# P x V of a head pair in one group of 32-column products on shared PSUM banks, with 64-row scores for the first three pairs

## The chip, the cores and the metric

The kernel runs on one core of one Trainium2 chip. The metric is the device time of one execution in microseconds (us); the time before is the median of three runs, 1092.33 us (1091.08 to 1095.45).

## The reference

Attention with a soft cap on the scores, then two feed-forward layers over all tokens, all in float32:

```python
scores = cap * np.tanh(scale * (q @ k.T) / cap)      # 4 x 12 heads, 448 tokens, 64 wide
attn = np.exp(scores - max); attn /= attn.sum(-1) + 1e-09
x = (attn @ v)  # heads side by side: 1792 x 768
h = x @ w_in                    # 768 -> 2048
x = (h * np.cos(h)) @ w_out     # 2048 -> 768
a = x @ w1; b = x @ w2          # 768 -> 1024 each
out = ((a * b) @ w3) @ w_out2   # 1024 -> 1024 -> 768
```

## The kernel before

The 48 heads are handled as 24 pairs; the two heads of a pair share one 128-row tile. The scores are computed transposed: keys lie on the partitions, in four chunks of 112, and the 448 queries along the free axis. TensorE multiplies in a one-pass float32 form, so an operand that needs full precision is split into a high and a low part. For that `a_load` loads each head's 64 rows of q and k twice, into the upper and the lower half of the partitions, and `a_split` makes of them `qh`, `ql` and `ks` (high part of k above, low part below), so that one product over 128 rows gives two terms at once. `c_S` makes two chunks of one head: two matmuls per chunk, into one of two double PSUM banks (`double`). `c_exp` runs tanh and exp on ScalarE, 112 x 896 each, into a `p` tile. `c_PV` takes the `p` tiles of both heads for half of the chunks: P x V with 64-column weights, the two heads in the two column halves of one bank, then the sums of the exponentials with a 32-column tile of ones, four side by side, in another bank. These products are plain float32; each stands as two instructions in the trace. `c_move` evicts both banks, `c_sums` sends the sums through DRAM to spread their reciprocals over the partitions, `c_norm` multiplies, and `a_out` splits the result for the first feed-forward layer.

Beside attention, TensorE computes `w3 @ w_out2` ahead of its use (`make_w34`, weights `w3h`, `w2h` and their low parts) and, later, the first layer (`moe1`). Those weights come as float64 words; `convert` turns them into float32: a scaling of the high words (line 861 on ScalarE or 862 on GpSimd, whichever the planner finds free), a step on GpSimd or DVE, then two bit operations on DVE (lines 874 and 878).

The order of all instructions is set by a planner (`Plan.schedule`): each step has a due time, the engines it may run on with a cost for each, and the buffers that it needs from rings. A ring hands its buffers out in the order in which its users were written down. For PSUM there are rings of two double banks for scores, one bank for P x V, one for the sums, and two (`hy_r`) for everything else. The order that the planner finds is then fixed for each engine; an instruction waits where what it needs is not there. One queue, SP's, issues all DMAs. All matmuls of `mm3` stand at lines 383 to 385, all tensor subtractions and additions of DVE at 369, copies at 359 (ScalarE) and 360 (DVE), DMAs at 379.

Of the kernel before, what the change touches and what calls it, by code (L numbers as in the profile page):

```python
# [11 lines left out]
F32 = mybir.dt.float32  # L12
# [7 lines left out]
P = 128  # L20
B, H, S, D = 4, 12, 448, 64
CP = 112
# [113 lines left out]
class Plan:  # L136
# [57 lines left out]
    def schedule(self):  # L194
# [23 lines left out]
        while done < len(self.ops):  # L218
# [4 lines left out]
            idle = {e for e in free if free[e] <= t + 1e-9}  # L223
            wait, rest, again = {}, [], False
            for c in cands:
# [6 lines left out]
                if pick[0] in idle and port(pick) and free["port"] > t + 1e-9:  # L232
                    pick = None
                elif pick[0] not in idle:
                    if len(o.opts) == 1:
                        wait[pick[0]] = wait.get(pick[0], 0.0) + pick[1] * PAR["back"]
                    pick = None
                if pick is None or any(it.slot is None and it.first is not o for it in o.uses if it.ring) or any(
                        it.ring.queue[0] is not it or not it.ring.free or it.ring.free[0][0] > t + 1e-9
                        for it in o.allocs):  # L240
                    rest.append(c)
                    continue
                for it in o.allocs:
                    it.ring.queue.pop(0)
                    it.slot = heapq.heappop(it.ring.free)[1]
# [88 lines left out]
def program(  # L334
# [70 lines left out]

    class Banks(Ring):
        def __init__(self, slots):
# [6 lines left out]
    class Doubles(Banks):  # L414
        def tile(self, k):
            return doubles[k]

    class Scratch:
# [7 lines left out]
        def at(self, sub, pick=None):  # L426
            return Ref(self.item, sub, pick)
# [76 lines left out]
    if general:  # L504
        tiles += [
            ("vr", [CP, NC, D], F32, 2), ("vs", [CP, NC, 2, D], F32R, 3), ("t", [CP, S], F32, G["nt"]), ("sm", [CP, 2, NC], F32, 4),
            ("rs", [CP, 2, NC], F32, 3), ("rb", [P, S], F32, 1),
            ("ph", [CP, S], F32R, G["nph"]), ("pl", [CP, S], F32R, G["npl"]),
        ]
    else:  # L510
        tiles += [("v", [CP, 2, NC, D], F32, 2), ("ones", [CP, Q], F32, 1)]
        tiles += [("p", [CP, 2, S], F32, 4), ("xs", [P, S], F32, 2), ("zs", [P, S], F32, 2), ("rs", [P, 2, S // D], F32, 2), ("rb", [P, S], F32, 1)]
    for tag, shape, dtype, n in tiles:
# [38 lines left out]

    def a_out(i, g):

        if i % 2 == 0:
            return
        b, h = divmod(i, H)
        kk = h // 2
        x = Ref(x32.pop(i // 2))
        if general:  # L560
            tt(at(g), x, Ref(rb.pop(i // 2)), x, S, ALU.mult, "PD")
# [6 lines left out]
        copy(at(g), th, x, S, "PAD")  # L568
        lo(at(g), tl, x, th, S)
        if b >= BH:  # L570
            for d, t in zip(xB_d, (th, tl)):
                z = d.at((b, kk), lambda d: d[b - BH, kk])
                dma(at(g + 1), z, t.view(lambda x: x.bitcast(F32)), r=[t], w=[z], kb=230, write=True)

# [17 lines left out]

    NT = NC // 2

    def c_consts():
# [11 lines left out]

    def c_S(i, c, g):
        qh, ql, ks = st[i]
        s = s_t[i, c] = s_r.ref()  # L610

        def f():
            for n in range(2):
                o, w = s()[:CP, n, :S], ks()[:, (2 * c + n) * CP:(2 * c + n + 1) * CP]
# [3 lines left out]
        plan.op(at(g), [("PE", 4 * MM, f)], r=st[i], w=[s])  # L618

    def c_exp(i, c, g):  # L620
        s = s_t.pop((i, c))[:CP, :, :S]
        p = ph_t[i, c] = A["p"].ref()
        for f, x, o in ((AF.Tanh, ts, s), (AF.Exp, pac, p)):
            plan.op(at(g), [("ACT", 0.144 + 2 * S / 1200,
                             lambda f=f, x=x, o=o: ACT.activation(o(), s(), f, scale=x[:CP]))],  # L625
                    r=[s], w=[o], table="exp")

    def c_PV(n, c, one, g):
        ps = [ph_t.pop((2 * n + j, c)) for j in range(2)]
        if c == 0:  # L630
            pv_t[n], zs_t[n] = pv_r.ref(), z_r.ref()
        pv, z, w = pv_t[n], zs_t[n], Ref(vt[n])
        flags = dict(start=c == 0, stop=c == NT - 1)
# [11 lines left out]
        plan.op(at(g), [("PE", 3 * 4 * MM, f)], r=[w, one, *ps], w=[pv, z])  # L645

# [26 lines left out]

    def c_norm(n, g):
        x32[n] = A["x32"].new()
        tt(at(g), Ref(x32[n]), pv_t.pop(n), Ref(rb[n]), S, ALU.mult, "DP")

# [5 lines left out]
    def columns():  # L683
        one = c_consts()
        a_load(0, -2)
        a_split(0, -1)
        for g in range(-8, NT * NH + 16):
            of_pair(a_load, -G["ql"], g, NT)
            of_head(cv_load, -2, g, NT)
            of_pair(a_split, -G["qs"], g, NT)  # L690
            if 0 <= g < NT * NH:
                n, k = divmod(g, 2 * NT)
                c, j = divmod(k, 2)
                c_S(2 * n + j, c, g)
                c_exp(2 * n + j, c, g)
# [8 lines left out]
        plan.move(pv_r, hy_r, at(g))  # L704
        plan.move(z_r, hy_r, at(g))

# [113 lines left out]
    def queries():  # L820
        a_load(0, -2)
        a_split(0, -1)
        for g in range(-8, NC * NH + 24):
# [14 lines left out]
            of_head(a_R, 8, g, NC)  # L838
            of_head(a_out, 17, g, NC)
            if g == NC * G["hsw"] + 11:  # L840
# [12 lines left out]

    def convert(due, raw_r, x, src, n):

# [26 lines left out]

    def f64(due, raw_r, x_r, src, n, hi, lw, spill=None):

        x = x_r.ref()[:, :n]
        convert(due, raw_r, x, src, n)
# [20 lines left out]
    def make_w34():  # L907
# [12 lines left out]
        for k, (fc, p) in enumerate(runs):  # L920
# [4 lines left out]
            w3 = pair(w3_r)  # L925
            f64(due - G["e3"] * (k == 0), raw_r, x_r, w3T[fc, :, p * F2:(p + 1) * F2], F2 // 2, *w3)
            for n, jc in enumerate(new):
                wo[jc] = pair(w2_r)
                f64(due - (G["e2"] - n * G["e1"]) * (k == 0), raw_r, x_r, w_out2[jc], DM, *wo[jc])
            for n in range(2):  # L930
# [423 lines left out]
```

## Time and profile before

| | before |
|---|---|
| median of three runs | 1092.33 us |
| the profiled execution, its own time | 1093.39 us |
| its span, first to last instruction | 1091.1 us |
| granted TensorE clock, mean share | 0.997 |
| busy: PE, DVE, ScalarE, GpSimd | 1064.5, 869.6, 502.1, 161.1 us |
| moved by DMA | 169.17 MB |

The page names TensorE's matmuls PE and its weight loads PEld, VectorE DVE, ScalarE ACT, GpSimd POOL. Matmuls overlap and their ends are modelled, so the step from one start to the next tells what a matmul costs, not its duration. In the window view, each stretch has busy time and number of instructions for each engine, the granted clock as a share of the full one, the busy share of the DMA engines and the rate in GB/s. In the timeline, a row has a start, a duration, what ran, and in brackets how long the engine was idle before it and what ended that.

### The profile page before, as it was taken

The numbers are of one execution on the slowest core, as the hardware profiler recorded it, in microseconds if no ns is written. First come the engines' busy times: TensorE is split into PE (matmuls) and PEld (weight loads), VectorE is DVE, ScalarE is ACT, GpSimd is POOL, SyncE is SP. The second block draws the span as 40 slices with busy tenths as digits, with TensorE's granted clock in tenths as the row PEclk, the third lists the DMA queues.
The fourth block names the chain that finished last, engine by engine and source line by source line (L and its number), as shares of the span: only waits on it lengthen the run. The fifth ranks groups of instructions, "written<-read, shape, count | busy, mean of one in ns | idle before, by whom it ended". The sixth has DMA issues, their size and how long they took to land.

```text
span 1091.1 us, 14889 instructions
## 1 busy us (share of the span) xinstructions
PE 1064.5 (98%) x5424; PEld 892.4 (82%) x5424; DVE 869.6 (80%) x1336; ACT 502.1 (46%) x661; POOL 161.1 (15%) x154
## 2 busy tenths in 40 slices
PE   5999999999999999999999999999999999999997
PEld 3666766677767777779999999998999999999996
DVE  6888767698978988969889977779799879667643
ACT  5788767787666656632244221112333236221121
POOL 2222111122312311111001110001223100000000
PEclk9999999999999999999999999999999999999999
DMA  8796876767756655425643422104655436321232
GB/s 244 200 221 181 231 209 174 219 208 223 219 161 197 188 171 166 153 84 193 223 141 119 147 58 59 58 15 136 223 188 203 141 104 226 119 87 59 59 96 95
DMA packets 83268, 169.17 MB, mean 155 GB/s; under 512 B 19698, under 2 KB 56562, under 8 KB 83186
## 3 DMA queue, kind: packets, MB, share of 16 engines
q1 hardware_dynamic: 83186, 168.14, 51.0%
q8 instruction: 44, 0.72, 0.3%
q14 instruction: 38, 0.31, 0.1%
HBM read 129.30 MB, written 38.62 MB: 154 GB/s over the span
## 4 chain that ended last, share of the span: by engine, by line
PE 90%; DVE 6%; ACT 2%; DMA 1%; issue 1%; SPq 0%; POOL 0%; DVEq 0%; POOLq 0%; ACTq 0%
PE bank L383 25%; PE bank L384 24%; PE bank L385 24%; PE bank L639 6%; PE double L615 3%; PE bank L643 3%; PE double L616 3%; DVE y L369 1%; DVE w L369 1%; DMA wi_d<-wx 1%; ACT double L625 1%; DVE kk L1008 0%; ACT p L625 0%; DMA kr<-in_k 0%; DVE g L369 0%
## 5 line engine op out<-in xcount | busy, mean ns | idle before, releaser
L383 PE MATMUL bank<-g,woh 128*128 128x448 f32 x384 | 140.8, 367 | 4.1 <-DVE y L369 3.5
L384 PE MATMUL bank<-g,woh 128*128 128x448 f32 x384 | 139.4, 363 | 0.9 <-DVE g L369 0.9
L383 PE MATMUL bank<-xh,wih 128*128 128x448 f32 x384 | 140.2, 365 | 0.0
L369 DVE TENSOR_TENSOR y<-bank,y 128x448 f32<-128x448 f32 x168 | 103.5, 618 | 45.7 <-PE bank L385 44.5
L385 PE MATMUL bank<-xh,wil 128*128 128x448 f32 x384 | 139.3, 363 | 0.0
L385 PE MATMUL bank<-g,wol 128*128 128x448 f32 x384 | 139.3, 363 | 0.0
L384 PE MATMUL bank<-xl,wih 128*128 128x448 f32 x384 | 139.2, 363 | 0.0
L359 ACT COPY hs<-bank 128x448 f32<-128x448 f32 x77 | 41.2, 535 | 200.9 <-PE bank L385 200.7
L625 ACT ACTIVATE double<-double,ts 112x896 f32<-112x896 f32 x96 | 94.0, 981 | 69.4 <-PE double L616 69.1
L625 ACT ACTIVATE p<-double,pac 112x896 f32<-112x896 f32 x96 | 96.6, 1012 | 1.8
L383 PEld LDWEIGHTS bank<-g,woh 128*128 128x128 f32 x384 | 71.9, 187 | 20.1 <-DVE y L369 6.2
L615 PE MATMUL double<-qh,ks 128*112 128x448 f32 x192 | 72.6, 378 | 13.9 <-DVE ks L369 9.6
L383 PEld LDWEIGHTS bank<-xh,wih 128*128 128x128 f32 x384 | 71.9, 187 | 16.0 <-issue 8.0
L639 PE MATMUL bank<-p,v 112*64 112x448 f32 x384 | 84.1, 558 | 0.0
L384 PEld LDWEIGHTS bank<-g,woh 128*128 128x128 f32 x384 | 72.1, 188 | 6.4 <-DVE g L369 1.3
L384 PEld LDWEIGHTS bank<-xl,wih 128*128 128x128 f32 x384 | 72.1, 188 | 5.2
L385 PEld LDWEIGHTS bank<-g,wol 128*128 128x128 f32 x384 | 72.1, 188 | 4.2
L385 PEld LDWEIGHTS bank<-xh,wil 128*128 128x128 f32 x384 | 72.1, 188 | 4.2
L616 PE MATMUL double<-ql,ks 128*112 128x448 f32 x192 | 72.3, 376 | 0.0
L384 PE MATMUL bank<-ab,w34h 128*128 128x448 f32 x192 | 69.7, 363 | 0.0
L383 PE MATMUL bank<-ab,w34h 128*128 128x448 f32 x192 | 69.7, 363 | 0.0
L385 PE MATMUL bank<-ab,w34l 128*128 128x448 f32 x192 | 69.3, 361 | 0.0
(224 smaller groups left out, 2304.4 us busy)
## 6 DMA issues: line engine op xcount, KB each, us to landing
rawc<-in_w_out SPq DMA_DIRECT2D x16, 768.0 KB, 5.1
stq<-w_d SPq DMA_DIRECT2D x32, 384.0 KB, 3.3
qr<-in_q SPq DMA_DIRECT2D x48, 224.0 KB, 4.2
kr<-in_k SPq DMA_DIRECT2D x48, 224.0 KB, 4.5
rawc<-in_w_in SPq DMA_DIRECT2D x13, 768.0 KB, 5.4
raw<-in_w3T SPq DMA_DIRECT2D x16, 512.0 KB, 5.9
rawl<-in_w SPq DMA_DIRECT2D x10, 768.0 KB, 4.7
raw<-in_w_out SPq DMA_DIRECT2D x8, 768.0 KB, 7.3
```

Of the source, the lines that this page charges most:

```text
L359: "A": ("ACT", (0.051 if psum else 0.094) + n / 1200, lambda: ACT.copy(dst(), src())),
L369: "D": ("DVE", 0.068 + n / 960, lambda: DVE.tensor_tensor(dst(), a(), b(), op=op))
L383: PE.matmul(out, wh, xh, start=first, stop=False, skip_group_check=on)
L384: PE.matmul(out, wh, xl, start=False, stop=False, skip_group_check=on)
L385: PE.matmul(out, wl, xh, start=False, stop=last, skip_group_check=on)
L615: PE.matmul(o, w, qh(), start=True, stop=False)
L616: PE.matmul(o, w, ql(), start=False, stop=True)
L625: lambda f=f, x=x, o=o: ACT.activation(o(), s(), f, scale=x[:CP]))],
L639: PE.matmul(pv()[j * D:(j + 1) * D, :S], w()[:, j, 2 * c + k], p()[:, k, :], **first)
L643: PE.matmul(z()[q:q + Q, :S], one(), p()[:, k, :], **flags)
```

## The change

`c_PV` takes the whole pair (both halves) as one step from pair 2 on; pairs 0 and 1 keep two halves. The P x V weights of a head are cut into two pieces of 32 columns, so that P x V and the sums have the same tile shape, four side by side. The banks of P x V and of the sums come from one ring of four with all other products (`hy_r`); that ring is "loose": a user may take a buffer out of the written order, if enough are free and no user with an earlier due time goes short. There are six `p` tiles in place of four. For the first three pairs (`SLIM`), q and k are loaded once, without the duplicate, and split at half the length; `c_S` then makes one chunk of both heads, three terms of 64 rows for each head, the heads in the two row halves and in the two banks of a double bank. The first weights' scaling may only run on GpSimd (`early`). Normalizing and its followers have other due times.

```diff
 class Ring:
+    loose = False
...
+                need = {}
+                for it in o.allocs:
+                    need[it.ring] = need.get(it.ring, 0) + 1
+                lack = {r for r, n in need.items() if sum(x[0] <= t + 1e-9 for x in r.free) < n}
                 if pick is None or any(it.slot is None and it.first is not o for it in o.uses if it.ring) or any(
-                        it.ring.queue[0] is not it or not it.ring.free or it.ring.free[0][0] > t + 1e-9
-                        for it in o.allocs):
+                        not r.loose and r.queue[0].first is not o for r in need) or lack or short & need.keys():
+                    short |= {r for r in lack if r.loose}
                     rest.append(c)
...
-        s_r, pv_r, z_r, hy_r = Doubles((0, 1)), Banks((4,)), Banks((5,)), Banks((6, 7))
+        s_r, hy_r = Doubles((0, 1)), Banks((4, 5, 6, 7))
...
-        tiles += [("p", [CP, 2, S], F32, 4), ...
+        tiles += [("p", [CP, 2, S], F32, 6), ...
...
+    SLIM = 3
+
+    def c_load(i, g):
+        if i // 2 >= SLIM:
+            return a_load(i, g)
+        b, h = divmod(i, H)
+        qk[i] = A["qr"].new(), A["kr"].new()
+        for it, src in zip(qk[i], (q2, k2)):
+            r = it.at(0, lambda t: t[:, 0])
+            dma(at(g) if i else -99.0, r, lambda src=src: src[b, h // 2], w=[r], kb=230)
+
+    def c_split(i, g):
...
+        copy(at(g), kh, k, S, "PAD")
+        lo(at(g), kl, k, kh, S)
+        copy(at(g), qh, q, S, "PAD")
+        lo(at(g), ql, q, qh, S)
+        st[i] = (kh, qh), (kh, ql), (kl, qh)
...
+    def c_S(n, k, g):
+        s = s_t[n, k] = s_r.ref()
+        if n < SLIM:
+            terms = st[2 * n]
+
+            def f():
+                for m, (w, x) in enumerate(terms):
+                    for j in range(2):
+                        r = slice(j * D, (j + 1) * D)
+                        PE.matmul(s()[:CP, j, :S], w()[r, k * CP:(k + 1) * CP], x()[r], start=m == 0, stop=m == 2)
...
-    def c_PV(n, c, one, g):
+    def c_PV(n, cs, one, g):
...
-            for k in range(2):
-                first = dict(start=c == 0 and k == 0, stop=c == NT - 1 and k == 1)
-                for j, p in enumerate(ps):
-                    PE.matmul(pv()[j * D:(j + 1) * D, :S], w()[:, j, 2 * c + k], p()[:, k, :], **first)
-            for j, p in enumerate(ps):
-                for k in range(2):
-                    q = Q * (2 * j + k)
-                    PE.matmul(z()[q:q + Q, :S], one(), p()[:, k, :], **flags)
+            for c in chunks:
+                flags = dict(start=c == 0, stop=c == NC - 1)
+                for q in range(P // Q):
+                    j, d = divmod(q * Q, D)
+                    PE.matmul(pv()[q * Q:(q + 1) * Q, :S], w()[:, j, c, d:d + Q], piece(j, c), **flags)
+            for c in cs:
+                for j in range(2):
+                    for k in range(2):
+                        q = Q * (2 * j + k)
+                        PE.matmul(z()[q:q + Q, :S], one(), piece(j, 2 * c + k), start=c == 0, stop=c == NT - 1)
...
-            if g >= 3 and g % 2 and g - 3 < NT * NH:
-                c_PV((g - 3) // (2 * NT), (g - 3) % (2 * NT) // 2, one, g)
+            of_two(lambda n, g: n < 2 and c_PV(n, [0], one, g), 3, g)
+            of_two(lambda n, g: c_PV(n, [1] if n < 2 else [0, 1], one, g), 5, g)
...
-            of_two(c_norm, 10, g)
-            of_head(a_out, 9, g, NT)
+            of_two(lambda n, g: c_norm(n, at(g) + 11), 6, g)
+            of_two(lambda n, g: a_out(2 * n + 1, at(g) + 14), 6, g)
...
-    def convert(due, raw_r, x, src, n):
+    def convert(due, raw_r, x, src, n, early=False):
...
-        ], r=[r], w=[r])
+        ][early:], r=[r], w=[r])
```

How the order moves shows at three places. In the names, the number behind a tile is its buffer; `bank_75` to `bank_78` are the four single banks, `double_82` and `double_83` the double ones.

TensorE, the P x V step of a pair after the start. Before, one half of pair 3, and the product behind it:

```order
L639 MATMUL bank_75<-p_153,v_128 64x448
L639 MATMUL bank_75<-p_157,v_128 64x448
L639 MATMUL bank_75<-p_153,v_128 64x448
L639 MATMUL bank_75<-p_157,v_128 64x448
L643 MATMUL bank_76<-p_153,ones_109 32x448 x2
L643 MATMUL bank_76<-p_157,ones_109 32x448 x2
L383 MATMUL bank_78<-w2h_210,w3h_159 128x384
```

In the changed kernel, the whole pair 2 (its sums stand as eight rows, of which two are shown):

```order
L694 MATMUL bank_77<-p_180,v_119 32x448 x4
L694 MATMUL bank_77<-p_196,v_119 32x448 x4
L694 MATMUL bank_77<-p_271,v_119 32x448 x4
L694 MATMUL bank_77<-p_276,v_119 32x448 x4
L699 MATMUL bank_78<-p_180,ones_109 32x448
L699 MATMUL bank_78<-p_196,ones_109 32x448
```

The two halves of a pair, which stood apart with other products between them, are one run of 16 and 8 products; all have 32 columns, and the banks are no longer always 75 and 76.

TensorE, around the first score tiles of pair 1. Before, the second pair of weight products stands ahead of them:

```order
L383 MATMUL bank_77<-w2h_210,w3h_159 128x384
L384 MATMUL bank_77<-w2l_226,w3h_159 128x384
L385 MATMUL bank_77<-w2h_210,w3l_171 128x384
L383 MATMUL bank_78<-w2h_210,w3h_159 128x384
L384 MATMUL bank_78<-w2l_226,w3h_159 128x384
L385 MATMUL bank_78<-w2h_210,w3l_171 128x384
L615 MATMUL double_82<-qh_205,ks_208 112x448
L616 MATMUL double_82<-ql_216,ks_208 112x448
```

In the changed kernel:

```order
L650 MATMUL double_83<-qh_202,ks_205 112x448 x2
L650 MATMUL double_83<-ql_226,ks_205 112x448 x2
L650 MATMUL double_83<-qh_202,ks_205 112x448 x2
L389 MATMUL bank_77<-w2h_223,w3h_165 128x384
L390 MATMUL bank_77<-w2l_247,w3h_165 128x384
L391 MATMUL bank_77<-w2h_223,w3l_176 128x384
L389 MATMUL bank_78<-w2h_223,w3h_165 128x384
L390 MATMUL bank_78<-w2l_247,w3h_165 128x384
L391 MATMUL bank_78<-w2h_223,w3l_176 128x384
L650 MATMUL double_82<-qh_202,ks_205 112x448 x2
```

The six weight products have moved behind the first two score tiles, to the place ahead of the third.

GpSimd, its first steps on weights (`raw` is what was loaded, `x` the converted tile). Before:

```order
L867 TENSOR_SCALAR x_143<-raw_115 128x512
L862 TENSOR_SCALAR raw_117<-raw_117 128x768
L867 TENSOR_SCALAR x_165<-raw_117 128x768
L862 TENSOR_SCALAR raw_119<-raw_119 128x768
L867 TENSOR_SCALAR x_143<-raw_119 128x768
L867 TENSOR_SCALAR x_165<-raw_115 128x768
```

In the changed kernel:

```order
L914 TENSOR_SCALAR raw_113<-raw_113 128x512
L919 TENSOR_SCALAR x_148<-raw_113 128x512
L914 TENSOR_SCALAR raw_115<-raw_115 128x768
L919 TENSOR_SCALAR x_167<-raw_115 128x768
L914 TENSOR_SCALAR raw_117<-raw_117 128x768
L919 TENSOR_SCALAR x_148<-raw_117 128x768
```

The scaling ahead of the first `x` step, which ScalarE did, now stands on GpSimd as well.

## Rows read from the trace of the kernel before

**Rows 1.** The page's table of engines: busy us, share of the span, instructions.

```profile
PE 1064.5 (98%) x5424; PEld 892.4 (82%) x5424; DVE 869.6 (80%) x1336; ACT 502.1 (46%) x661; POOL 161.1 (15%) x154
```

**Rows 2.** Busy time by stretch, from two questions to the window view.

```profile
0.00:45.00 45.00, 30.33 (x135) 17.52 (x136) 29.89 (x40) 27.74 (x37) 11.88 (x15) 0.96 0.80 229
45.00:200.00 155.00, 155.00 (x867) 105.66 (x869) 118.47 (x181) 118.62 (x146) 25.56 (x29) 1.00 0.77 199
200.00:490.00 290.00, 285.69 (x1468) 214.41 (x1460) 248.21 (x368) 188.78 (x216) 64.63 (x57) 1.00 0.60 183
...
225.00:255.00 30.00, 29.98 (x155) 23.46 (x154) 28.29 (x41) 25.42 (x32) 7.36 (x6) 1.00 0.76 233
```

**Rows 3.** Timeline of PE around one P x V block.

```profile
164.56 0.34 PE L385 MATMUL bank<-w2h,w3l 128*128 128x384 f32 x1
164.83 1.72 PE L639 MATMUL bank<-p,v 112*64 112x448 f32 x8
166.48 0.96 PE L643 MATMUL bank<-p,ones 112*32 112x448 f32 x8
167.37 0.45 PE L383 MATMUL bank<-w2h,w3h 128*128 128x384 f32 x1
167.65 0.34 PE L384 MATMUL bank<-w2l,w3h 128*128 128x384 f32 x1
167.83 0.34 PE L385 MATMUL bank<-w2h,w3l 128*128 128x384 f32 x1
```

**Rows 4.** Timeline inside the same block, weight loads, and one piece of PE.

```profile
165.26 0.14 PEld L639 LDWEIGHTS bank<-p,v 112*64 112x64 f32 x2 [0.23 <-issue]
165.63 0.14 PEld L639 LDWEIGHTS bank<-p,v 112*64 112x64 f32 x2 [0.23 <-issue]
...
166.01 0.55 PE L639 MATMUL bank<-p,v 112*64 112x448 f32 x2
...
166.48 0.15 PEld L643 LDWEIGHTS bank<-p,ones 112*32 112x32 f32 x7 [0.70 <-issue]
```

**Rows 5.** Timeline of the start, all engines.

```profile
1.19 1.38 SPq L379 DMA_DIRECT2D qr<-in_q  x2
...
5.79 0.63 DVE L360 CAST qh<-qr 128x896 fp32r<-128x896 f32 x1 [1.38 <-DMA qr<-in_q]
...
7.81 0.63 DVE L360 CAST ks<-kr 128x896 fp32r<-128x896 f32 x1 [0.27 <-DMA kr<-in_k]
8.48 1.09 DVE L369 TENSOR_TENSOR ks<-kr,ks 64x896 fp32r<-64x896 f32 x1
...
9.62 0.72 PE L615 MATMUL double<-qh,ks 128*112 128x448 f32 x1 [9.62 <-DVE ks L369]
10.02 0.67 ACT L861 ACTIVATE raw<-raw 128x512 f32<-128x512 f32 x1 [5.37 <-DMA raw<-in_w3T]
...
10.51 0.58 PE L615 MATMUL double<-qh,ks 128*112 128x448 f32 x1
...
10.88 0.58 PE L616 MATMUL double<-ql,ks 128*112 128x448 f32 x1
...
11.49 0.98 ACT L625 ACTIVATE double<-double,ts 112x896 f32<-112x896 f32 x1 [0.81 <-PE double L616]
```

**Rows 6.** Timeline of PE in the stretch of pair 1.

```profile
26.15 0.45 PE L384 MATMUL bank<-w2l,w3h 128*128 128x384 f32 x1 [0.97 <-DVE w2l L369]
...
27.57 0.36 PE L616 MATMUL double<-ql,ks 128*112 128x448 f32 x1
27.77 0.37 PE L615 MATMUL double<-qh,ks 128*112 128x448 f32 x1
...
31.24 0.45 PE L615 MATMUL double<-qh,ks 128*112 128x448 f32 x1 [2.09 <-ACT p L625]
...
33.81 2.64 PE L639 MATMUL bank<-p,v 112*64 112x448 f32 x8
```

**Rows 7.** Waits of PE from 200 to 490 us: total, times, longest.

```profile
PE bank L383 <- DVE y L369: 3.5, 5, 1.2
```

More of the change, by code (lines that the diff above doesn't have):

```diff
@@ L223, in schedule @@
             idle = {e for e in free if free[e] <= t + 1e-9}
-            wait, rest, again = {}, [], False
+            wait, rest, again, short = {}, [], False, set()
             for c in cands:
@@ L243, in schedule @@
                 for it in o.allocs:
-                    it.ring.queue.pop(0)
+                    it.ring.queue.remove(it)
                     it.slot = heapq.heappop(it.ring.free)[1]
@@ L406, in program @@
     class Banks(Ring):
+        loose = not general
         def __init__(self, slots):
@@ L551, in a_split, with a_out @@
             st[i + j] = qh[:, j], ql[:, j], ks[:, j]
-    def a_out(i, g):
+    def a_out(i, due):
         if i % 2 == 0:
@@ L560, in a_out @@
         if general:
-            tt(at(g), x, Ref(rb.pop(i // 2)), x, S, ALU.mult, "PD")
+            tt(due, x, Ref(rb.pop(i // 2)), x, S, ALU.mult, "PD")
         if b < BH:
@@ L567, in a_out @@
             th, tl = A["xsh"].ref(), A["xsl"].ref()
-        copy(at(g), th, x, S, "PAD")
-        lo(at(g), tl, x, th, S)
+        copy(due, th, x, S, "PAD")
+        lo(due, tl, x, th, S)
         if b >= BH:
@@ L572, in a_out @@
                 z = d.at((b, kk), lambda d: d[b - BH, kk])
-                dma(at(g + 1), z, t.view(lambda x: x.bitcast(F32)), r=[t], w=[z], kb=230, write=True)
+                dma(due + 3, z, t.view(lambda x: x.bitcast(F32)), r=[t], w=[z], kb=230, write=True)
     def of_head(f, lag, g, n):
@@ L593, in program @@
     NT = NC // 2
+    SLIM = 3
[8 more added lines that the diff above has]
+    def c_split(i, g):
+        if i // 2 >= SLIM:
+            return a_split(i, g)
+        q, k = (x.at(0, lambda t: t[:, 0]) for x in qk.pop(i))
+        qh, ql, ks = (A[x].new() for x in ("qh", "ql", "ks"))
+        kh, kl = (ks.at(j, lambda t, j=j: t[:, j]) for j in range(2))
+        qh, ql = (x.at(0, lambda t: t[:, 0]) for x in (qh, ql))
+        copy(at(g), kh, k, S, "PAD")
[3 more added lines that the diff above has]
+        st[i] = (kh, qh), (kh, ql), (kl, qh)
     def c_consts():
@@ L606, in cv_load, with c_exp @@
         dma(at(g), r, lambda: v[b, h], w=[r])
-    def c_S(i, c, g):
-        qh, ql, ks = st[i]
-        s = s_t[i, c] = s_r.ref()
+    def c_S(n, k, g):
[7 more added lines that the diff above has]
+                        PE.matmul(s()[:CP, j, :S], w()[r, k * CP:(k + 1) * CP], x()[r], start=m == 0, stop=m == 2)
+            plan.op(at(g), [("PE", 3 * MM + 0.3, f)], r=[y for x in terms for y in x], w=[s])
+            return
+        c, j = divmod(k, 2)
+        qh, ql, ks = st[2 * n + j]
         def f():
-            for n in range(2):
-                o, w = s()[:CP, n, :S], ks()[:, (2 * c + n) * CP:(2 * c + n + 1) * CP]
+            for m in range(2):
+                o, w = s()[:CP, m, :S], ks()[:, (2 * c + m) * CP:(2 * c + m + 1) * CP]
                 PE.matmul(o, w, qh(), start=True, stop=False)
                 PE.matmul(o, w, ql(), start=False, stop=True)
[L618 to L622, printed above, removed]
+        plan.op(at(g), [("PE", 4 * MM, f)], r=st[2 * n + j], w=[s])
+    def c_exp(n, k, g):
+        s = s_t.pop((n, k))[:CP, :, :S]
+        p = A["p"].ref()
+        for j in range(2):
+            if n < SLIM:
+                ph_t[n, j, k] = p, j
+            else:
+                ph_t[n, k % 2, k // 2 * 2 + j] = p, j
         for f, x, o in ((AF.Tanh, ts, s), (AF.Exp, pac, p)):
@@ L626, in c_exp, with piece @@
                     r=[s], w=[o], table="exp")
-    def c_PV(n, c, one, g):
-        ps = [ph_t.pop((2 * n + j, c)) for j in range(2)]
-        if c == 0:
-            pv_t[n], zs_t[n] = pv_r.ref(), z_r.ref()
+    def c_PV(n, cs, one, g):
+        chunks = range(2 * cs[0], 2 * cs[-1] + 2)
+        ps = {(j, c): ph_t.pop((n, j, c)) for j in range(2) for c in chunks}
+        if 0 in cs:
+            pv_t[n], zs_t[n] = hy_r.ref(), hy_r.ref()
         pv, z, w = pv_t[n], zs_t[n], Ref(vt[n])
-        flags = dict(start=c == 0, stop=c == NT - 1)
+        def piece(j, c):
+            p, m = ps[j, c]
+            return p()[:, m, :]
         def f():
-            for k in range(2):
-                first = dict(start=c == 0 and k == 0, stop=c == NT - 1 and k == 1)
-                for j, p in enumerate(ps):
-                    PE.matmul(pv()[j * D:(j + 1) * D, :S], w()[:, j, 2 * c + k], p()[:, k, :], **first)
-            for j, p in enumerate(ps):
-                for k in range(2):
-                    q = Q * (2 * j + k)
-                    PE.matmul(z()[q:q + Q, :S], one(), p()[:, k, :], **flags)
-        plan.op(at(g), [("PE", 3 * 4 * MM, f)], r=[w, one, *ps], w=[pv, z])
+            for c in chunks:
[4 more added lines that the diff above has]
+            for c in cs:
+                for j in range(2):
+                    for k in range(2):
+                        q = Q * (2 * j + k)
+                        PE.matmul(z()[q:q + Q, :S], one(), piece(j, 2 * c + k), start=c == 0, stop=c == NT - 1)
+        plan.op(at(g), [("PE", 12 * len(cs) * MM + 0.3, f)], r=[w, one, *{x.item: x for x, _ in ps.values()}.values()], w=[pv, z])
     def c_move(n, g):
@@ L881, in convert, with f64 @@
         plan.op(due - 5, [("DVE", 0.07 + n / 960, low, True)], r=[r, x], w=[x])
[L883 removed]
+    def f64(due, raw_r, x_r, src, n, hi, lw, spill=None, early=False):
         x = x_r.ref()[:, :n]
[L886 removed]
+        convert(due, raw_r, x, src, n, early)
         if spill is not None:
```

29 lines of the change are left out of this document (13 added, 16 removed).

## The prediction

> **What bounds the kernel now.** I read the page's table of engines first: TensorE (PE) is busy for 98% of the span, and no other engine for more than 80% [rows 1]. Since that is an average, the stages come next. From 45 to 200 us PE has no idle time at all, from 200 to 490 us it lacks 4.3 us of 290, and the first 45 us lack 14.7 us [rows 2]. So there are two prices. After 45 us a microsecond of work taken from PE is a microsecond off the end, as long as the others keep up; VectorE (DVE) has 118 of 155 us there and then 248 of 290. Before 45 us it is the chain of loads, splits and exponentials that counts, and PE's work is partly free.
>
> The third view is PE's timeline around one P x V block [rows 3], with the weight loads inside it [rows 4]; it shows what a block costs beyond its columns. The fourth is the start of the program [rows 5], the fifth the gaps in the second pair's stretch [rows 6], the last the waits [rows 7].
>
> **P x V in one group.** Today one half of a pair goes from the start of the product before it (164.56) to the second start after it (167.65): 3.09 us. An ordinary step of the products around it is 0.18 (167.65 to 167.83), so the half block itself takes 3.09 - 2 x 0.175 = 2.74 us [rows 3]. The groups of matmuls that run side by side start 0.375 apart (165.26, 165.63, 166.01) [rows 4]: four groups of two for P x V (each product is two instructions in the trace) and two groups of four for the sums, 6 x 0.375 = 2.25 us. The other 0.49 us is what goes with the change of tile shape: 0.10 to enter (164.83 - 164.56 less a step), 0.05 in the first group, whose loads are not hidden (0.43 in place of 0.375), 0.10 between 64 and 32 columns (166.01 to 166.48 is 0.47), 0.14 in the sums and their leaving (0.89 for two groups), 0.10 until the next product is back in step (167.37 to 167.65).
>
> After the change the weights of P x V are 32 columns wide. A pair has 16 products of twice two instructions, four side by side: 8 groups, as today, and 4 groups for the sums, as today. That a group of four takes 0.375 as well is an assumption; the nearest row is the sums, which run four side by side today and whose two groups take 0.89 with the leaving [rows 3], their eight loads starting together (seven end within 0.15) [rows 4]. A whole pair then costs 12 x 0.375 + 0.10 + 0.14 + 0.10 = 4.84 us in place of 2 x 2.74 = 5.48: 0.64 us less. 22 of the 24 pairs go whole: **-14.1 us**. Pairs 0 and 1 keep two halves and lose the first-group cost and the inner change, 0.15 each: 4 x 0.15 = **-0.6 us**. The bounds: nothing if each group of four pays what an exposed load costs today (12 x 0.055 = 0.66 a pair), -15 us if the sums' leaving is shorter too. I take -14.7, because the sums are the same shape.
>
> **The start.** The first product waits until 9.62 for a chain: two q loads, two k loads, a cast and a subtraction on each [rows 5]. With one load for two heads, the k load is second in the queue after the constant, where the second q load is now, with the same bytes; both q loads have landed by 5.79. DVE's four steps halve in length (0.63 and 1.09 over 896 elements, so about 0.33 and 0.56 over 448). Cast and subtraction of k end 0.9 us after 5.8, and the first product starts near 6.9: **-2.7 us**. It is on the path, as nothing else is ready for PE. The tanh starts 1.87 us after it (11.49); with three steps of 0.37 (10.51 to 10.88) in place of four, where two heads' matmuls run side by side, twice in the chain of the first pair, that is **-0.8 us**. In the stretch of pair 1, PE waits 0.97 us for the low part of a weight, and 2.09 us for an exponential, between the second and third score tile [rows 6]. The new order puts six weight products (6 x 0.175 = 1.05 us) into just that second gap. I count both the 0.97 and 1.05 as filled: **-2.0 us**. Behind the 2.09 us of idleness the eight P x V instructions take 2.64 us [rows 6] in place of 1.72 [rows 3], in a stretch in which the granted clock is not whole (0.96 over 0 to 45 us, so part of it at 1.2 of the two levels 1.2 and 2.4 GHz) [rows 2]; with the gap halved I count half of the 0.92: **-0.5 us**. The start gives **-6.0 us**; its bounds are -2.7 (the first product alone) and -7.5 (both gaps and the slow stretch gone).
>
> **Scores of 64 rows.** Before: 16 steps of 0.20 a pair (27.57 to 27.77) [rows 6]. After: 24 matmuls in 12 steps, 0.8 us less, if two run side by side, 24 steps or 1.6 us more if not. No row shows two row halves at work together; I take side by side, from the column tiles in [rows 4]. But each block also enters and leaves another tile shape, at about 0.35 us by the parts above; pair 1 has two such blocks and pair 2 four, between weight products. 6 x 0.35 - 2 x 0.8 = **+0.5 us** (pair 0 is in the start). Bounds: -1.6 and +5.3.
>
> **Edits that I count at nothing.** GpSimd takes the first scaling from ScalarE (0.67 at 10.02, [rows 5]): the step keeps about its length and is followed by a GpSimd step already; ScalarE's 0.67 would now stand just before an earlier tanh, so it may give up to 0.7. If GpSimd were late, the weight products behind it would be, and the two w2 gaps of the start would open again (those 2 us are the price). Six DMAs fewer, 1.4 MB, shorten SP's queue and the loads of the first 45 us. P's six buffers only hold P for longer. Normalizing and the writes of its result are due earlier; their cover is the pairs that follow, and nothing on PE reads them before the second layer. Sharing the banks gives the weights two more banks between blocks, and costs them none: during a block they have two, as now. It could cost waits (a rival) or take away some of the 3.5 us that PE waits for the `y` sums on DVE [rows 7]; I count neither.
>
> **Keeping up.** PE's pairs from 200 to 490 us become 0.64 us shorter while DVE is at 248 of 290 and, from 225 to 255, at 28.3 of 30 [rows 2]. DVE gets 595 instructions in place of 582; at 0.63 for a cast that is 8 us at most, and six of the casts and subtractions are of half length. The DMA share of 0.77 and ScalarE's 119 of 155 us [rows 2] leave room. I give back **+1 us** for that: bounds 0 and +5.
>
> **Sum:** -14.7 - 6.0 + 0.5 + 1.0 = -19.2 us against this execution's own 1093.39, which is 1.06 above the median of 1092.33: about **1073** on the scale of the median.
>
> **Rivals.**
> 1. *DVE sets the pace from 200 to 490 us.* For: the 28.3 of 30, and the only waits of PE there are for DVE. Against: they are 3.5 us in all. Half of eleven pairs' 0.64 us is lost, and the `y` waits double: +3.5 + 3.5 - 1: about 1079. Chance 0.17.
> 2. *The 64-row halves do not run side by side.* Pairs 1 and 2 then cost 2 x 2.4 us more than forecast, and the first pair 0.8 to 1.5 in its chain: 1079 as well. For: no row shows it. Chance 0.13.
> 3. *The loads of P x V come into the open.* The Trainium skill, "TensorE: Matmul & The Clock Gate", Part 3 on row and column tiling, says that a weight load overlaps a matmul in flight only where their row groups differ, and all of these use the same rows. By that rule 12 groups pay an exposed load. As a mechanism of this kernel: 0.055 a group, 0.66 us a pair, which eats the gain: 1093.4 - 6.0 + 0.5 = 1087.9, 1087 by the median. The trace speaks against it: the loads at 165.26 and 165.63 run while matmuls on the same rows do, and the groups keep 0.375 [rows 4]. Chance 0.03.
> 4. *Slower: P x V waits for banks.* It now asks for two free banks of the four at once, and evictions on ScalarE and DVE that stand behind other work decide when it gets them. Before, its two were its own, and PE never waited for them. PE's longest single wait for an eviction is 1.2 us [rows 7]. It takes 19/22 = 0.9 us a pair to undo the gain; at 1.2 a pair 22 x 1.2 = 26 us: 1073 + 26 = 1099. Against it: a block's banks are evicted while weights use the other two. Chance 0.04.
> 5. *More than forecast:* the waits for DVE disappear with the extra banks (-3.5) and the start gives its 7.5: about 1068. Chance 0.10.
>
> The forecast has the remaining 0.53. The change does what it says in any case: the new order has the 32-column products and the pairs whole.
>
> **From cases to numbers.** The range runs from below case 5 to above cases 1 and 2 with the bounds of their terms: 1064 to 1085. A measurement of this kernel tells about 0.5%, 5.5 us, from no change, so faster is below 1086.9: the forecast, cases 1, 2 and 5, less some of their upper tail, 0.91; within, case 3 and that tail, 0.05; slower 0.04.
>
> **What would show it.** Right: L694 and L699 groups starting 0.375 to 0.38 apart with no 0.47 between them; some 4.84 us a pair; the first product near 6.9; pairs of 64-row matmuls whose starts lie a few ns apart, 0.2 a step; the second gap of pair 1 near 1 us; PE without idle time from 45 to 200 us. Wrong: groups of 0.43 or more; row halves 0.2 apart each; PE waits for DVE or ScalarE of over 8 us from 200 to 490 us, or any before L694 on an eviction.

## The result, and the profile after

The changed kernel takes 1067.26 us (median of four runs, 1065.92 to 1068.79) against 1092.03 us in the same comparison: a ratio of 0.9768, 95% interval 0.9742 to 0.9794. The forecast was 1073 us, with a range of 1064 to 1085. The profiled execution took 1065.92 us with a span of 1064.1 us, so 27.5 us less than the profiled execution of before.

The page's table of engines after, to be held beside [rows 1]:

```profile
PE 1045.1 (98%) x5832; PEld 894.5 (84%) x5832; DVE 874.0 (82%) x1343; ACT 492.1 (46%) x649; POOL 173.6 (16%) x159
```

The windows of [rows 2], and one more from a question of its own:

```profile
0.00:45.00 45.00, 34.90 (x232) 20.79 (x234) 36.88 (x52) 30.34 (x40) 16.91 (x20) 1.00 0.77 224
45.00:200.00 155.00, 151.87 (x1060) 107.89 (x1057) 124.40 (x195) 113.60 (x138) 31.06 (x31) 1.00 0.76 208
200.00:490.00 290.00, 290.00 (x1708) 233.84 (x1707) 264.80 (x391) 184.11 (x213) 70.61 (x59) 1.00 0.62 189
...
255.00:285.00 30.00, 30.00 (x174) 24.44 (x174) 29.90 (x43) 21.40 (x23) 8.97 (x8) 1.00 0.70 212
```

Three things changed. From 200 to 490 us PE now has no idle time, where it lacked 4.3 us, although DVE is at 29.9 of 30 us in the tightest stretch. From 45 to 200 us PE lacks 3.1 us, where it lacked none. In the first 45 us it is idle for 10.1 us in place of 14.7, and the stretch at half the clock behind 32 us is gone. The 1.00 of the view does not show the very start: up to 12 us the score products step by 0.37 us in both kernels, where later ones step by 0.20, so they run at the lower of the two levels.

The waits of PE after (total, times, longest), for [rows 7]:

```profile
PE double L650 <- DVE ks L366: 5.9, 1, 5.9
PE double L650 <- ACT p L675: 3.0, 2, 2.0
PE double L660 <- ACT p L675: 3.0, 1, 3.0
PE double L650 <- DVE ql L375: 1.2, 1, 1.2
PE bank L391 <- DVE w3l L375: 0.2, 1, 0.2
```

L650 is a 64-row score product, so three of these lie in the start. The waits for `y` are gone; the 3.0 us before L660 and the 0.2 us for `w3l` (at 48 us) are new, after the start.

One P x V block after, PE, for [rows 3]:

```profile
167.65 0.37 PE L661 MATMUL double<-ql,ks 128*112 128x448 f32 x1
167.94 3.21 PE L694 MATMUL bank<-p,v 112*32 112x448 f32 x32
170.97 1.69 PE L699 MATMUL bank<-p,ones 112*32 112x448 f32 x16
172.59 0.44 PE L389 MATMUL bank<-w2h,w3h 128*128 128x384 f32 x1
172.87 0.34 PE L390 MATMUL bank<-w2l,w3h 128*128 128x384 f32 x1
```

Its weight loads, for [rows 4]:

```profile
168.35 0.13 PEld L694 LDWEIGHTS bank<-p,v 112*32 112x32 f32 x4 [0.25 <-issue]
168.72 0.13 PEld L694 LDWEIGHTS bank<-p,v 112*32 112x32 f32 x4 [0.25 <-issue]
...
170.22 0.13 PEld L694 LDWEIGHTS bank<-p,v 112*32 112x32 f32 x4 [0.25 <-issue]
170.60 0.13 PEld L699 LDWEIGHTS bank<-p,ones 112*32 112x32 f32 x4 [0.25 <-issue]
```

From 167.65 to 172.87 are 5.22 us; less a score step of 0.20 and a product step of 0.175 the block costs 4.85 us. Groups of four start 0.375 apart (168.35 to 168.72), and so do P x V and the sums (170.22 to 170.60), where the shape no longer changes.

The start, for [rows 5]:

```profile
4.46 0.39 DVE L366 CAST qh<-qr 128x448 fp32r<-128x448 f32 x1
...
4.89 0.63 DVE L375 TENSOR_TENSOR ql<-qr,qh 128x448 fp32r<-128x448 f32 x1
5.43 0.39 DVE L366 CAST ks<-kr 128x448 fp32r<-128x448 f32 x1
...
5.87 0.71 PE L650 MATMUL double<-qh,ks 64*112 64x448 f32 x2 [5.87 <-DVE ks L366]
6.38 0.58 PE L650 MATMUL double<-ql,ks 64*112 64x448 f32 x2
...
7.37 2.10 ACT L675 ACTIVATE double<-double,ts 112x896 f32<-112x896 f32 x2 [2.59 <-PE double L650]
```

The first product waits for the cast of k alone, since the first of the three terms needs only high parts, and each row holds the two row halves (x2), which start 3 to 7 ns apart.

The rest of the start, PE in the stretch of pair 1, for [rows 6]:

```profile
21.64 0.46 PE L650 MATMUL double<-ql,ks 64*112 64x448 f32 x2 [1.17 <-DVE ql L375]
...
22.34 0.37 PE L650 MATMUL double<-ql,ks 64*112 64x448 f32 x2
22.55 0.37 PE L650 MATMUL double<-qh,ks 64*112 64x448 f32 x2
...
25.20 0.46 PE L650 MATMUL double<-qh,ks 64*112 64x448 f32 x2 [1.02 <-ACT p L675]
...
26.91 1.71 PE L694 MATMUL bank<-p,v 112*32 112x448 f32 x16
```

Where PE waited 0.97 and 2.09 us it waits 1.17 and 1.02, 0.9 us less, and the step of two row halves at the whole clock is 0.21 us (22.34 to 22.55). The weights' gap is filled, but a new one of 1.17 for the low part of q stands there.

Where the one new wait comes from, in the timeline of several engines:

```profile
147.93 1.25 POOL L919 TENSOR_SCALAR x<-raw 128x768 f32<-128x768 f32 x1
...
156.10 0.54 SPq L385 DMA_DIRECT2D wi_d<-x  x1
...
160.59 1.72 POOL L919 TENSOR_SCALAR x<-raw 128x768 f32<-128x768 f32 x2 [11.41 <-DMA rs_d<-rs]
...
161.50 1.62 DVE L926 SCALAR_TENSOR_TENSOR x<-raw,x 128x768 uint32<-128x768 uint32 x1 [3.94 <-POOL x L919]
...
163.04 0.61 DVE L375 TENSOR_TENSOR x<-xs,rb 128x448 f32<-128x448 f32 x1
...
163.69 0.56 ACT L365 CAST xh<-x 128x448 fp32r<-128x448 f32 x1 [3.94 <-DVE x L375]
164.16 0.97 ACT L675 ACTIVATE double<-double,ts 112x896 f32<-112x896 f32 x1
...
166.95 0.46 PE L660 MATMUL double<-qh,ks 128*112 128x448 f32 x1 [2.96 <-ACT p L675]
```

GpSimd stands still for 11.4 us before it converts a weight. The profile names `rs_d` as what ended that, but GpSimd also writes an `x` buffer, of which there are two, and the store of one, `wi_d<-x`, was issued at 156.10. The trace decides for the store: it landed after 4.4 us, at 160.46, on the semaphore for which GpSimd's queue stands in one wait at L919 from 147.30 to 160.49; `rs_d<-rs` landed at 160.62, when the conversion had begun. Behind GpSimd waits DVE's bit operation (3.94 us), behind that, in DVE's order, normalizing (163.04), behind that ScalarE's `xh` (3.94 us), and behind `xh` the tanh and exp on which PE's next scores wait (166.95). An idle queue off the critical path reaches PE through two others that stand in order.

### The profile page after: what moved, and what is told of

Read it like the earlier page. It is cut to its first block, busy times and chain, and to the rows that moved or that the text cites. A ratio compares the mean times of both kernels' runs of the same rounds, so it can differ in the third digit from the quotient of the medians.

```text
span 1064.1 us, 15654 instructions
## 1 busy us (share of the span) xinstructions
PE 1045.1 (98%) x5832; PEld 894.5 (84%) x5832; DVE 874.0 (82%) x1343; ACT 492.1 (46%) x649; POOL 173.6 (16%) x159
## 4 chain that ended last, share of the span: by engine, by line
PE 93%; DVE 2%; issue 2%; DMA 1%; ACT 1%; SPq 0%; POOL 0%; DVEq 0%; ACTq 0%; POOLq 0%
PE bank L389 26%; PE bank L391 26%; PE bank L390 26%; PE bank L694 6%; PE double L660 3%; PE bank L699 3%; PE double L661 3%; DMA kr<-in_k 1%; DMA raw<-in_w3T 0%; DVE x L930 0%; SPq L385 0%; DVE x L926 0%; DVE ks L375 0%; DVE ql L375 0%; ACT double L675 0%
## 5 line engine op out<-in xcount | busy, mean ns | idle before, releaser
L694 PE MATMUL bank<-p,v 112*32 112x448 f32 x768 | 78.7, 549 | 0.0
L660 PE MATMUL double<-qh,ks 128*112 128x448 f32 x168 | 61.5, 366 | 3.0 <-ACT p L675 3.0
L661 PE MATMUL double<-ql,ks 128*112 128x448 f32 x168 | 61.3, 365 | 0.0
```

The source lines that it names most:

```text
L694: PE.matmul(pv()[q * Q:(q + 1) * Q, :S], w()[:, j, c, d:d + Q], piece(j, c), **flags)
```

## Experiments

Ratios are to the kernel before, with 95% intervals; its median was 1092.0 to 1092.4 us in all comparisons. The order of all engines is planned anew for each variant, so an edit moves more than its own lines.

**The shape of P x V (e1).** Whole pairs as in the change, but 64-column weights:

```diff
-                for q in range(P // Q):
-                    j, d = divmod(q * Q, D)
-                    PE.matmul(pv()[q * Q:(q + 1) * Q, :S], w()[:, j, c, d:d + Q], piece(j, c), **flags)
+                for j in range(2):
+                    PE.matmul(pv()[j * D:(j + 1) * D, :S], w()[:, j, c], piece(j, c), **flags)
```

> The changed kernel with 64-column weights in P x V again, the whole pair still one step, the order the same. If tile shapes are what a block pays (theory 1): the first group takes 0.43 in place of 0.40 and the step from P x V to the sums 0.47 in place of 0.375, 0.125 us a block, 26 blocks: 3.3 us slower than the changed kernel, about 1070.5. If four loads a group had cost something as well (rival), the groups would now be shorter than 0.375 and the time would stay or fall: 1067 or less.

Measured: 1072.29 us, ratio 0.9813 (0.9797 to 0.9829). In the two profiles the steps of P x V and the sums are 6.5 us longer together. About 4.0 us of that is shape: the median block of a whole pair costs 5.01 us in place of 4.85, and one of a half 2.74 in place of 2.59 (0.156 and 0.15 a block, where 0.125 was expected). 1.7 us is a stretch of 3.4 us at half the clock behind the 3.0 us wait, which stands here too, and most of the rest a wait of 0.9 us for `v` in the start. So the narrow weights are worth some 4 us of PE's work, and the 5.0 us between the medians hold the slow stretch as well.

**Whole pairs (e2).** Two halves for every pair, in 32 columns:

```diff
-            of_two(lambda n, g: n < 2 and c_PV(n, [0], one, g), 3, g)
-            of_two(lambda n, g: c_PV(n, [1] if n < 2 else [0, 1], one, g), 5, g)
+            of_two(lambda n, g: c_PV(n, [0], one, g), 3, g)
+            of_two(lambda n, g: c_PV(n, [1], one, g), 5, g)
```

> The changed kernel with two halves for every pair. Theory 1 (entering and leaving a block costs 0.34 to 0.36 us): 22 blocks more, 7.7 us slower than the changed kernel, about 1075. Rival (the long block holds up the scores and with them ScalarE, so that the halves win some of it back): 1070 or less, with fewer waits of PE for exponentials than the 3.0 us that the changed kernel has near 167 us.

Measured: 1071.53 us, 0.9805 (0.9789 to 0.9821). A block more costs 0.34 us (two halves of 2.60 in place of 4.85), 22 of them 7.5 us; PE's last product starts only 5.6 us later, mainly because the 3.0 us wait is not there in this order (PE is busy for 155.00 of 155 us from 45 to 200).

**The start (e3, e10).** `SLIM = 3` set to 0, and to 1:

> The changed kernel without the shorter loads and the 64-row scores of the first three pairs. Theory 1 (the start chain): the first product goes back from 5.87 to 9.6 and the whole start, measured at the fourth set of weight products (8.2 us earlier in the changed kernel), goes back by 5 to 7 us: about 1073. Rival (the start is lost again later, since DVE and the loads set the pace up to 200 us): 1069 or less, with PE idle after 45 us in the changed kernel where here it is not.

Measured with 0: 1077.35 us, 0.9856 (0.9839 to 0.9873). The first product starts at 10.93, 1.3 us later than in the kernel before, since k's load landed late. The lag against the changed kernel is 4.9 us from 49 to 107 us and 5.4 from 129 to 160. The rest of the 11.1 us between the profiles (by PE's last start) comes later: a wait of 2.2 us near 172, where the changed kernel has its own of 3.0, and one of 1.8 us near 277, each with a half-clock stretch of 3.4 us behind it. So the 10.1 us between the medians are not the price of the start alone.

> The halved loads and 64-row scores for pair 0 alone; pairs 1 and 2 as in the kernel before. Theory (the start's gain is that of pair 0, the first product at 5.9 us; the 64-row scores of pairs 1 and 2 cost about half a microsecond by their change of tile shape): 1066 to 1068, first product at 5.9. Rival (the six DMAs fewer of pairs 1 and 2 matter too, as they free the queue for weights): 1069 to 1074, with waits for v, k or weights in the first 45 us.

Measured with 1: 1073.92 us, 0.9833 (0.9814 to 0.9852). The rival's numbers came, for half of its reason. The first product starts at 6.11. Then PE waits 0.9 us for `w2l`, 0.5 for `ks` and 2.1 for `p` before 28 us, and is 1.8 us behind the changed kernel from 49 to 107 us, 1.6 to 160: that much the slim pairs 1 and 2 are worth in their own stage. The rest is mainly a wait of 1.9 us for `zs` at 272 us, with a half-clock stretch behind it.

**Own banks, the rest kept (e4).** The edit gives P x V and the sums back their own rings:

```diff
-        s_r, hy_r = Doubles((0, 1)), Banks((4, 5, 6, 7))
+        s_r, pv_r, z_r, hy_r = Doubles((0, 1)), Own((4,)), Own((5,)), Banks((6, 7))
...
-            pv_t[n], zs_t[n] = hy_r.ref(), hy_r.ref()
+            pv_t[n], zs_t[n] = pv_r.ref(), z_r.ref()
```

(`Own` is a `Banks` with `loose = False`; once attention is over, both banks go to `hy_r`, as before.)

> The changed kernel with one bank for P x V and one for the sums again, in written order, and two for the rest; all else as changed. Theory 2 (the extra banks took away the waits of PE for the y sums on DVE, 3.5 us from 200 to 490 us, and one of 0.9 near 760): these waits come back, 4 to 5 us slower, about 1072, and more if a block now waits for the eviction of the block before it. Rival (they went because the order shifted): no waits for y above 1 us in all, 1067 to 1069.

Measured: 1076.62 us, 0.9869 (0.9842 to 0.9896), 9.4 us slower than the changed kernel. Its waits of PE after 45 us:

```profile
PE bank L389 <- DVE sum L375: 3.0, 1, 3.0
PE bank L389 <- DVE y L375: 2.9, 3, 1.4
PE bank L389 <- DVE y L366: 1.5, 2, 1.0
```

From 200 to 490 us PE waits 4.4 us for `y` again, and 3.0 us for a `sum` at 160 us. By PE's last start the two profiles differ by 8.8 us, of which 8.0 arise from 200 to 490 us.

**Shared banks alone (e9).** The changed kernel with `SLIM = 0`, 64-column weights, halves, and the early scaling free, so the kernel before with shared loose banks, six `p` tiles and the other due times of normalizing:

> The kernel before with the shared banks (and six P tiles) alone: 64-column weights, halves, duplicated loads, scaling as before. Theory 2 (the extra banks take away the waits for DVE's y sums whatever the block is): 4.4 us of waits gone, 1087 to 1088. Rival (the shared banks only undo what the long block with its own banks costs): 1091 to 1093.

Measured: 1083.08 us, 0.9902 (0.9880 to 0.9923), 9.3 us faster. The windows of this run:

```profile
45.00:200.00 155.00, 155.00 (x870) 105.54 (x868) 117.67 (x182) 115.51 (x142) 25.48 (x29) 1.00 0.73 198
200.00:490.00 290.00, 290.00 (x1503) 222.09 (x1496) 259.79 (x385) 184.17 (x212) 66.07 (x57) 1.00 0.58 183
```

Up to 190 us each product starts within 0.25 us of the kernel before, and from there to 490 us the lead grows to 7.2 us, to 8.8 us after 760. From 45 us to the end the list of PE's waits is empty, where the kernel before has, beside [rows 7]:

```profile
PE bank L384 <- DVE g L369: 0.9, 1, 0.9
PE bank L383 <- DVE y L360: 0.5, 1, 0.5
```

The whole gain lies in the stretches where PE waited for `y` and `g`, and is more than the waits. Steps of PE after 190 us that lie outside P x V blocks and are over 0.212 us exceed 0.20 us by 11.4 us in all before (52 steps) and by 2.8 us here (25): 8.6 us, of which the waits that the profile lists are 4.9. The others are waits too short for that list, and the second step after each, 0.31 us in place of 0.20. The 2.8 us that are left are all such second steps behind P x V blocks. The due times and `p` tiles by themselves do not do it, since e4 and e11 keep both and have the waits for `y`. That the ring is loose and that it has four banks were not tried apart.

**P x V alone (e11).** Whole pairs in 32 columns on their own banks (e4's lines), `SLIM = 0`, the early scaling free; the six `p` tiles and the due times of normalizing stay:

> The forecast's main term by itself: P x V of whole pairs in 32-column pieces, on the two banks of its own that the kernel before had, with its loads and scores of the start and its scaling. Theory (the forecast's term is 14.7 us and needs no sharing of banks): about 1077 to 1078 against 1092, P x V and the sums 14 us shorter on TensorE. Rival (without sharing, the waits for VectorE take the gain back): 1082 to 1088, with TensorE waiting for sums or y in the trace for 6 us or more.

Measured: 1084.99 us, 0.9925 (0.9907 to 0.9943). The rival's time came, and waits of its kind. The waits of PE:

```profile
PE bank L389 <- DVE sum L375: 4.2, 1, 4.2
PE bank L389 <- DVE y L375: 3.4, 4, 1.4
PE bank L389 <- DVE y L366: 2.0, 3, 1.0
```

The longest one, in the timeline of PE:

```profile
170.54 0.69 PE L389 MATMUL bank<-w2h,w3h 128*128 128x384 f32 x1 [4.24 <-DVE sum L375]
171.03 0.52 PE L390 MATMUL bank<-w2l,w3h 128*128 128x384 f32 x1
171.35 0.52 PE L391 MATMUL bank<-w2h,w3l 128*128 128x384 f32 x1
```

The chain ahead of it, on GpSimd and DVE:

```profile
162.48 0.54 SPq L385 DMA_DIRECT2D wi_d<-x  x1
...
167.77 0.86 POOL L924 TENSOR_SCALAR x<-raw 128x768 f32<-128x768 f32 x1 [12.02 <-DMA wi_d<-x]
...
168.67 1.35 DVE L931 SCALAR_TENSOR_TENSOR x<-raw,x 128x768 uint32<-128x768 uint32 x1 [5.06 <-POOL x L924]
169.94 0.55 DVE L375 TENSOR_TENSOR sum<-bank,sum 128x384 f32<-128x384 f32 x1
```

The same store of an `x` buffer holds GpSimd, and DVE behind it; this time the eviction of a bank stands behind them. After it PE steps by 0.32 us in place of 0.175: the granted clock is at half, 1.2 GHz, for 6.8 us. P x V and the sums themselves are 10.2 us shorter on PE by their steps, and 14.6 us with the 22 entries and leavings that are gone (0.20 us each): the term of the forecast is there, and 9.5 us of it are given back in this profile, which is of the slowest of the four runs (7.2 us by the medians). Little of that is `y`, for which PE waited before as well: its long steps after 190 us exceed 0.20 us by 10.8 us, where the kernel before has 10.0 without the leavings that are gone here. The one wait for `sum` (4.2), the half clock behind it (3.4) and a wait for `p` at 142 us (1.2) are the rest. Nor do shared banks alone make the cut count: with `SLIM = 0` in both, whole pairs in 32 columns take 5.7 us off the kernel with shared banks (e3 against e9, which differ in the early scaling too), since e3 has its later load (1.3) and the two waits with their half-clock stretches (7.4 together).

**The third x buffer (e8).** `nx=2` to 3, and `w2bufs=6` to 5 for the room:

> A third x buffer (and five w2 buffers in place of six, for the room). Theory (the one new wait of the changed kernel, 3.0 us near 167 us, comes from GpSimd waiting for an x buffer until a spill has landed): the wait is gone, and with it the half-clock stretch that follows it in some runs, 1063 to 1065 against 1067. Rival (the transfer is late for another reason, the DMA rate): the wait stays or moves, 1066 to 1069.

Measured: 1070.42 us, 0.9801 (0.9772 to 0.9831). DVE no longer stands still near 160 us, and the long wait for `p` is gone, which bears out the theory of its cause; but PE waits for `zs` (1.6 us at 160.6, 1.0 at 227), for `p` (1.2 at 208) and for `xl` (0.6 at 217) in its place. The time is 3.2 us above that of the changed kernel: nothing was gained, and since `w2` has one buffer fewer, the run does not show the third buffer's effect alone.

**Row halves in series (e5).** The loops over terms and heads in `c_S` exchanged:

```diff
-                for m, (w, x) in enumerate(terms):
-                    for j in range(2):
+                for j in range(2):
+                    for m, (w, x) in enumerate(terms):
```

> The changed kernel with its 64-row products in another sequence: all three of the first head, then all three of the second, so that the two row halves meet only at the seam (5 steps a chunk in place of 3); the order of everything else is the same. Theory 1 (side by side is what makes 64 rows affordable): 2 steps more in 4 chunks of pair 0 at 0.37 us and in 8 of pairs 1 and 2 at 0.2 us, 6.2 us of TensorE's work, of which ScalarE's pace in pairs 0 and 1 hides up to 2: 4 to 6 us slower than the changed kernel, about 1072. Rival (the seam order does not matter, since TensorE waits for ScalarE there anyway): 1068 or less.

Measured: 1068.72 us, 0.9779 (0.9757 to 0.9801): no difference from the changed kernel. The timeline of PE shows why:

```profile
5.88 0.71 PE L650 MATMUL double<-qh,ks 64*112 64x448 f32 x1 [5.88 <-DVE ks L366]
6.39 0.57 PE L650 MATMUL double<-ql,ks 64*112 64x448 f32 x1
6.54 0.80 PE L650 MATMUL double<-qh,ks 64*112 64x448 f32 x2
7.05 0.57 PE L650 MATMUL double<-ql,ks 64*112 64x448 f32 x1
```

The row of two at 6.54 is the second head's first product (6.54) and the first head's third (6.76), which stands ahead of it in the order. The heads run as two streams, 5.88, 6.39, 6.76 and 6.54, 7.05, 7.43: behind its first product each steps by 0.37, as both do in the changed kernel, and the one at 7.43 is the one that reports the end of the chunk. So the edit did not put them in series, and the price of serial halves stays untested.

**The two edits counted at nothing (e6, e7, c2).** The scaling free for ScalarE or GpSimd (`[early:]` taken away), four `p` tiles in place of six, and both:

> The changed kernel with the first weights' scaling free to run on ScalarE or GpSimd again. Forecast: nothing, up to 0.7 us at the first tanh. Rival (ScalarE's time in the first 45 us is what the step buys): 2 us or more, seen as a later fourth set of weight products (32.9 in the changed kernel). Expected: 1067 to 1069.

> The changed kernel with four P tiles again. A whole pair holds all four until its block is done. Forecast (P's six buffers only hold P for longer, worth nothing): 1067 to 1070. Rival (they are the condition of the whole pair): the next pair's exponentials cannot start before the block ends, ScalarE stands for some 3 us in each of 22 pairs, and TensorE waits for scores where its other products run out: 1075 to 1090.

> Both edits that the forecast counts at nothing taken back together: four P tiles and the early scaling free for ScalarE or GpSimd. Theory (worth nothing each, so together as well): 1066 to 1068, a ratio within 0.3% of the changed kernel's. Rival (each covers for the other): 1071 or more, with TensorE waiting for P tiles or weights.

Measured: 1066.10 us, 0.9756 (0.9734 to 0.9777); 1066.11 us, 0.9752 (0.9733 to 0.9772); and together 1075.69 us, 0.9848 (0.9830 to 0.9865). Each alone is worth nothing, as forecast. Together they cost 8.4 us, which is the rival's time, but not mainly by its waits for P tiles or weights: PE waits 2.3 us for a `sum` at 161 us behind a standstill of DVE like the one above (4.2 us for GpSimd), with a half-clock stretch behind it, and 2.5 us for `zs` in four pieces. Here 22 of 24 `zs` evictions are DVE's, in place of 4; but so are 21 in the run with four tiles alone. Why both are needed for the loss stays open. No variant is faster than the changed kernel by more than the intervals can tell.

## Why the prediction came out right, and which step did not

**P x V, −14.7: right.** A whole pair costs 4.85 us where 4.84 was forecast, because a group of four P x V products takes the 0.375 of the sums. PE's steps of P x V and the sums are 10.6 us shorter in sum, and the 22 entries and leavings that are gone add 4.4: 15.0 in all. The account below takes the forecast's 14.7. This is work taken from PE; what it gives in time hangs on the waits (e11, e3).

**The start, −6.0, and the scores, +0.5: right in size, with other parts.** The first product came at 5.87, not 6.9: its one q load had landed by 4.46, where two took until 5.79, and the product needs no subtraction (−3.75 in place of −2.7; the forecast's own steps, 5.79 and 0.9 and the 0.05 between subtraction and product, give 6.75). The tanh follows after 1.50 us, as forecast (1.87 less 0.4). Of the 2.0 us of gaps 0.9 were gained. The half-clock stretch between 32 and 46 us is gone (the window view of before has a granted clock of 0.88 for these 14 us, so 1.7 us of work; I had 0.5). Row halves run side by side at 0.20 to 0.21 a step, and a block enters and leaves for 0.39, where I had 0.35. What the rest of the account leaves for start and scores together is −6.0 against my −5.5 (−5.7 with the 15.0 above). It is a remainder, and no run measures it by itself: e3 gives 4.9 us in the start's own stage, 1.3 of them by its later load.

**Shared banks, counted at nothing: the step that failed.** The text said that sharing "could cost waits (a rival) or take away some of the 3.5 us that PE waits for the `y` sums on DVE"; "I count neither". Alone it is worth 9.3 us (e9), taking it out costs 9.4 (e4), and between e11 and e3 it is 7.6 (with the early scaling): about a third of the whole gain. I had its mechanism in rival 5, but priced it by the listed waits of one line. After 190 us the excess steps outside P x V fell from 11.4 to 1.4 us; 1.4 us of that are leavings of blocks that are gone, which e9 still had, and 8.6 us are the banks'.

**Keeping up, +1: inside its bounds by luck.** No wait for DVE from 200 to 490 us came of the shorter pairs, so its mechanism did not act. One wait of 3.0 us came at 167 us, from an `x` buffer whose store had not landed, which no term of mine had. The 595 and 582 instructions of DVE in this term stand in no row; the page's tables have 1343 and 1336.

The account of the two profiles, by PE's last start (1084.1 to 1058.0 us, −26.2): −14.7 P x V, −8.6 banks, +3.1 the new wait with its slower restart; −6.0 remains for the start and the scores. The forecast had −14.7, 0, +1, −5.5. So the time lay 6 us under the forecast by the banks, less what the new wait took back, and inside the range only because the range began below rival 5.

**The rivals.** DVE setting the pace (1): false here, PE is full where DVE has 29.9 of 30 us. With the banks missing, PE waits for `y` again, 4.4 us in e4 and 5.4 in e11, which is not twice the 4.0 of before. Row halves not side by side (2): false. Loads in the open (3): false; the rule of the Trainium skill named there ("TensorE: Matmul & The Clock Gate", Part 3), by which loads overlap only where row groups differ, taken by that sentence alone, disagrees with this trace: loads of four at 168.35 and 168.72 run beside products on the same rows, and groups keep 0.375. P x V waiting for banks (4): false, no wait of PE in front of L694 on an eviction. More than forecast (5): the time came (1068 forecast, 1067.3 measured), with more from the banks than its 3.5 us and less from the start than its 7.5, so its number came partly by luck.

## What to carry to other kernels

Where the busiest engine waits for evictions, price a change of its buffers by the sum of all its long steps, less those that only change the tile shape, not by the listed waits of one line: here 4.9 us of listed waits were worth 8.6. A cut of the busiest engine's work need not come out in the time: P x V alone gave 7.4 of its 14.6 us (e11), and 5.7 on shared banks without the short start (e3 against e9), because one or two waits of 2 to 4 us, with the half clock that can follow them, take back what many blocks have saved. With a planner that sets the order, one edit moves waits elsewhere (a standstill of 9 to 12 us on GpSimd came out as nothing on TensorE in e9, and as 4.2 us in e11), so differences of some us between variants say little about the edited line.

## What the runs showed that I had not expected

- Products in the two row halves of TensorE ran out of the written order, each half in its own (e5: 6.54 before 6.76).
- After a wait of 1.8 to 4.2 us the granted clock fell to half for 3.4 or 6.8 us in some runs, and not in others: behind the 3.0 us of the changed kernel's profile it stayed whole, behind the same wait in e1 it fell, at 1.7 us of work.
- k's first loads landed 1.3 us later in e3 than in the kernel before (the cast of k at 9.12, not 7.81), though SP issued the same loads ahead of them, at the same times.
